# Weight parts in three steps, with the power of two moved into the casts, and shifted event times, in a fused gated-linear-attention and squared-ReLU kernel

## The chip, the cores and the metric

The kernel runs on one NeuronCore of a Trainium2 chip. The metric is device time in microseconds for one execution; a row of runs gives a median. The profile shown is of one execution of its own. TensorE does the matmuls, VectorE (DVE) and ScalarE (ACT) the elementwise work, SyncE (SP) issues all DMAs.

## The reference

Four batches of eight heads run a recurrence over 768 steps with a 48 x 48 state per head; the outputs of the eight heads side by side are the 384 columns of x (3072 tokens), which goes through a feed-forward layer with squared ReLU. q, k, v and alpha are float32; the two weight matrices come as 64-bit floats, which the kernel turns into float32 itself (L153 to L182, `first`, `middle`, `second`).

```python
state = alpha[:, :, t, :, None] * state + np.einsum('bhd,bhe->bhde', k[:, :, t], v[:, :, t])
y[:, :, t] = np.einsum('bhd,bhde->bhe', q[:, :, t], state)
...
x = np.ascontiguousarray(attn_out.transpose(0, 2, 1, 3)).reshape(B * S, H * D)
...
h = np.maximum(x @ w_in, 0.0)       # 384 -> 2048
return (h * h @ w_out)              # 2048 -> 384
```

## The kernel before

**Work.** The sequence is cut into chunks of 128 steps. A block is one chunk of one batch: 24 blocks. Four blocks (one chunk of all batches) make a group of 512 tokens: groups 0 to 5. Attention is done for two blocks at a time ("a pair"), in a chunked form: logs of alpha (`ln`), their split into two fp32r parts (`sp`), a cumulative sum by matmul (`cs`), exponentials (`eb`, `ei`), products with q and k (`mq`, `mk`), transposes on TensorE (`turn`), copies to SBUF (`qc`, `kc`), then `ga` and `gb`: scores, state sums, masks (`am`), new states (`us`, `st`, lines 406 to 421) and the outputs y of the pair before. `bl` writes the last row of the decay to DRAM and `br` reads it back turned, as `last`, which L421 needs.

**Feed-forward in three fp32r passes.** Group 0 uses plain float32 matmuls for its first layer and most of its second. From then on each operand is split in two parts, and three passes replace one float32 product. With E = 2^-12 and NEAR = 1 - 2^-13, a weight piece W (128 x 768 words, 8 pieces `i` of w_in, 8 pieces `o` of w_out) becomes b = fp32r(W NEAR) on ScalarE (`cast_w`, L551), l = W - b on VectorE (`rest_w`, through `combine`, L547), l / E on ScalarE (`scale_w`, L565), d = b - l/E on VectorE (`diff_w`, L547). b stays in SBUF; l and d go to DRAM (`keep`, L556) and are read back for each later group (`pump`, L589). Of the activations, x or the hidden values, a = fp32r(x NEAR) on ScalarE and l = x - a on VectorE (`split_to`, L596 and L547), d = l - E a on VectorE (`diff_to`, L600). A sum in PSUM takes b a and l l, is scaled by 1 + E (or E times it is added later), and then takes d d.

In the first layer (`layer_in`) 16 slices j give `in_x(j)` (six matmuls) and, two slices later, `in_y(j)` (three). A string of letters says by j mod 4 where the rest of a slice is done: D is one activation that scales by E, an add and a squared ReLU on VectorE; A is scaling, ReLU and square on ScalarE; M is A with the square on VectorE. The second layer (`layer_out`) is a row of `out_x(n)` (eight matmuls) and `out_y`; in groups 0 and 1 a part of it is done with plain float32 weights (`out_plain`).

**Order.** The first 36 us are a written-out list of steps. From there on `weave` takes a list of units of TensorE's work, each with a cost (1.05 for `in_x`, 0.53 for `in_y`, 1.08 for `out_x`, 1 for `out_plain`), and a list of events with times in the same units; an event is issued ahead of the first unit that begins at or after its time. The table `AT` (L19) holds these times: `g0`, `g1`, `g` when a pair's attention begins (in groups 0, 1, later), `sc0` how far group 0's events are stretched, `ga`, `gb` their place within a pair, `w_first`, `w_in_at`, `w_in_by`, `o0`, `o2` when weight pieces are split, `wstep` the distance of the steps of one split, `gx`, `g0x`, `g1x`, `xs` the split of the next x, `s0`, `h0`, `h1`, `h1by` where splits of hidden values stand, `str1` when the reads of d pieces begin, `tp`, `tp1` the letters. Each engine runs its instructions in the order of issue. PSUM is one pool of eight banks for everything; weight pieces share 26 buffers of SBUF.

`prepare` makes the events of one piece:

```python
def prepare(at, w, p):
    step = AT["wstep"]
    fs = (cast_w, rest_w, scale_w, diff_w)
    return [(at + i * step, f, (w, p)) for i, f in enumerate(fs)]
```

Of the kernel before, what the change touches and what calls it, by code (L numbers as in the profile page):

```python
# [9 lines left out]
FP32 = mybir.dt.float32  # L10
FP32R = mybir.dt.float32r
U32 = mybir.dt.uint32
AF = mybir.ActivationFunctionType
ALU = mybir.AluOpType
# [1 line left out]


GB = 4
AT = {'evs': 0.4, 'lead': 4, 'post': 3, 'w_first': (46.0, 49.5, 53.0), 'wstep': 1.6, 'w_in_at': 2, 'w_in_by': 3.4, 'room1': 22, 'room': 25, 's0': 4, 'ahead': 6, 'late': 2, 'xs': 0.2, 'g0': (-0.5, 19.5, 28.0), 'sc0': (2.35, 2.35, 2.35), 'g1': (2.5, 19.5, 35.0), 'g': (2.2, 15.0), 'g1x': 50, 'gx': 46, 'g0x': 55.5, 'k0': 2, 'h0': 18, 'k1': 4, 'h1': 4, 'h1by': 2, 'evs0': 0.8, 'tp': 'ADMD', 'tp1': 'ADAD', 'split': 8, 'o0': (40, 47), 'o1': (), 'o2': (23, 26, 29, 35, 42, 36), 'str1': 24, 'ga': 10, 'gb': 12.5}  # L19


RUN = {0: 128, 32: 32, 64: 64, 96: 32}
# [3 lines left out]
def kernel(  # L26
# [12 lines left out]
    nc = tc.nc  # L39
# [44 lines left out]
    def wt(name, dt=FP32, shape=(KM, DF // NW)):  # L84
        return wt_pool.tile([128, *shape], dt, tag="wt", name=name)
# [161 lines left out]

    SPLIT = AT["split"]

# [279 lines left out]
    E = 2.0**-12  # L529
    NEAR = 1.0 - 2.0**-13  # L530
# [3 lines left out]
    whole = {"i": w_in, "o": w_out}  # L534
# [5 lines left out]
    here, todo, room = {}, [], [22]  # L540
# [4 lines left out]
    def combine(steps):  # L545
        for o, x, op, z in steps:
            nc.vector.tensor_tensor(out=o, in0=x, in1=z, op=op)  # L547

    def cast_w(w, p):
        b = here["b", w, p] = wt("wb", FP32R, shapes[w])  # L550
        nc.scalar.activation(out=b, in_=whole[w][p], func=AF.Copy, scale=NEAR)  # L551

    made, stored, cut = {}, set(), set()

    def keep(x, w, p):
        nc.sync.dma_start(out=kept_parts[x, w, p], in_=words(made[x, w, p]))  # L556
        stored.add((x, w, p))

    def rest_w(w, p):
        l = made["l", w, p] = wt("wl", FP32R, shapes[w])  # L560
        combine(((l, whole[w][p], ALU.subtract, here["b", w, p].bitcast(FP32)),))

    def scale_w(w, p):
        l = made["l", w, p]
        nc.scalar.activation(out=l, in_=l.bitcast(FP32), func=AF.Copy, scale=1.0 / E)  # L565
        keep("l", w, p)

    def diff_w(w, p):
        b, l = here["b", w, p].bitcast(FP32), made["l", w, p].bitcast(FP32)
        d = made["d", w, p] = wt("wd", FP32R, shapes[w])  # L570
        cut.add((w, p))
        combine(((d, b, ALU.subtract, l),))
        keep("d", w, p)
        for x in "ld":
            t = made.pop((x, w, p))
            if w == "i" or p >= NW - AT["k0"] or (x == "l" and p >= NW - AT["k1"]):
                here[x, w, p] = t
        pump()

    def prepare(at, w, p):  # L580
        step = AT["wstep"]
        fs = (cast_w, rest_w, scale_w, diff_w)
        return [(at + i * step, f, (w, p)) for i, f in enumerate(fs)]

    def pump():
        while todo and todo[0] in stored and len(here) + len(made) + 2 * NW - len(cut) < room[0]:
            key = todo.pop(0)
            here[key] = wt("w" + key[0], FP32R, shapes[key[1]])
            nc.sync.dma_start(out=words(here[key]), in_=kept_parts[key])  # L589
# [3 lines left out]
        pump()  # L593

    def split_to(a, l, x):
        nc.scalar.activation(out=a, in_=x, func=AF.Copy, scale=NEAR)  # L596
        combine(((l, x, ALU.subtract, a.bitcast(FP32)),))

    def diff_to(d, a, l):
        nc.vector.scalar_tensor_tensor(  # L600
            out=d, in0=a.bitcast(FP32), scalar=-E, in1=l.bitcast(FP32), op0=ALU.mult, op1=ALU.add
        )

    def raw_r(name):
        return raw_pool.tile([128, KM, GB * C], FP32R, tag="raw", name=name)
# [3 lines left out]
    def split_x(g, kk):  # L609
        if kk == 0:  # L610
            x_parts["x"], x_parts["a"], x_parts["l"] = xT.pop(g), raw_r("xa"), raw_r("xl")
        split_to(x_parts["a"][:, kk], x_parts["l"][:, kk], x_parts["x"][kk])

    def diff_x(g, kk):
        if kk == 0:
            x_parts["d"] = raw_r("xd")
        diff_to(*(x_parts[k][:, kk] for k in "dal"))
# [44 lines left out]
    def splits_of_x(at, g):  # L662
        return [(at + i * AT["xs"], f, (g, i % KM)) for i, f in enumerate((split_x,) * KM + (diff_x,) * KM)]

    def layer_in(g):
        units = []
        for n in range(NJ + 2):
            if n < NJ:
                units.append((1.05, in_x, (n,)))
            if 0 <= n - 2 < NJ:  # L670
                units.append((0.53, in_y, (n - 2,)))
            if 0 <= n - AT["post"] < NJ:
                units.append((0, in_post, (n - AT["post"],)))
            if AT["lead"] <= n < AT["lead"] + AHEAD and (g > 1 or AT["k1"] == NW):
# [6 lines left out]
    def split_h(n, i):  # L681
        r = i % (AHEAD + MORE)
        if r < AHEAD:
            a, l = two_k("ha", FP32R), two_k("hl", FP32R)
        else:
            if i == AHEAD:
                extra[:] = [raw_r("hx") for _ in range(3)]
            x = 2 * (r - AHEAD)
            a, l = (extra[y // 3][:, y % 3] for y in (x, x + 1))
        split_to(a, l, hid.pop(n))  # L690
        h_parts[n] = a, l

    def diff_h(n):
        h_diff[n] = two_k("hd", FP32R)
        diff_to(h_diff[n], *h_parts[n])
# [250 lines left out]
    for p, at in enumerate(AT["w_first"]):  # L946
        events += prepare(at, "i", p)
# [6 lines left out]
    for p, at in enumerate(AT["o0"]):  # L954
        events += prepare(at, "o", order[p])
# [18 lines left out]
    for g in range(1, NG):  # L974
        events = []
        if g + 1 < NG:
            n = GB * (g + 1) + 2
            *ts, t0, t1 = AT["g1" if g == 1 else "g"]
            pairs = [(t, n - 2, False) for t in ts] + [(t0, n, True), (t1, n + 2, True)]
            events += attention(pairs, 1)  # L980
            events += splits_of_x(AT["g1x" if g == 1 else "gx"], g + 1)
        if g == 1:
            m = len(AT["w_first"])
            for p in range(m, NW):
                events += prepare(AT["w_in_at"] + AT["w_in_by"] * (p - m), "i", p)
            for i, at in enumerate(AT["o1"] + AT["o2"]):
                events += prepare(at, "o", order[len(AT["o0"]) + i])
            n = min(AT["k0"], AT["k1"])
            todo.extend(("l", "o", p) for p in range(NW - n, NW))
            events.append((AT["str1"], stream_out, (AT["k1"], "d")))  # L990
        kinds[0] = AT["tp1" if g == 1 else "tp"]
        room[0] = AT["room1" if g == 1 else "room"]
        events.append((26, stream, (g + 1,)))
        events.sort(key=lambda x: x[0])
        weave(layer_in(g) + layer_out(g), events)
        if g == 1:
            w_out.clear()
            hid.clear()
            acc.clear()
# [30 lines left out]
```

## Time and profile before

| | |
|---|---|
| median of 3 runs | 523.02 us (522.5 to 523.05) |
| span of the profiled execution | 520.6 us |
| granted TensorE clock | 1.000 |
| ScalarE scaling of `wl`, L565 | 16 x 847 ns, 13.5 us |
| ScalarE cast of weights, L551 | 16, 13.4 us |
| VectorE `wl` and `wd`, L547 | 32, 30.4 us |
| ScalarE `xa`, `ha`, `hx`, L596 | 91, 53.6 us |
| group 1, about 128 to 217 us | VectorE busy 14 to 18 of 20 us in its stages, ScalarE 8 to 18 |

The lines of the page give the busy time of an engine, the mean of one instruction, and the idle time ahead of it with what ended it. A line number can be that of a helper: L547 is `combine`, whoever calls it. "issue" is idle time for which the profile shows no cause.

### The profile page before, as it was taken

The numbers are of one execution on the slowest core, as the hardware profiler recorded it, in microseconds if no ns is written. First come the engines' busy times: TensorE is split into PE (matmuls) and PEld (weight loads), VectorE is DVE, ScalarE is ACT, GpSimd is POOL, SyncE is SP. The second block draws the span as 40 slices with busy tenths as digits, with TensorE's granted clock in tenths as the row PEclk, the third lists the DMA queues.
The fourth block names the chain that finished last, engine by engine and source line by source line (L and its number), as shares of the span: only waits on it lengthen the run. The fifth ranks groups of instructions, "written<-read, shape, count | busy, mean of one in ns | idle before, by whom it ended". The sixth has DMA issues, their size and how long they took to land.

```text
span 520.6 us, 12925 instructions
## 1 busy us (share of the span) xinstructions
PE 510.8 (98%) x5276; PEld 418.2 (80%) x5276; DVE 366.0 (70%) x631; ACT 313.0 (60%) x650; POOL 5.4 (1%) x29
## 2 busy tenths in 40 slices
PE   7989999999999999999999999999999999999997
PEld 4754455668887668988899988899988899988997
DVE  4798989979978787867597476587465476363861
ACT  4668785677888594575963275963275763164620
POOL 4000000000000000000000000000000000000000
PEclk9999999999999999999999999999999999999999
DMA  9999687244686787898884788964673534898201
GB/s 161 209 278 213 196 240 218 60 114 176 224 200 196 195 246 198 264 317 206 195 248 148 251 246 198 230 187 150 231 255 126 179 126 151 268 340 293 70 0 62
DMA packets 140995, 102.36 MB, mean 197 GB/s; under 512 B 111476, under 2 KB 114568, under 8 KB 140936
## 3 DMA queue, kind: packets, MB, share of 16 engines
q1 hardware_dynamic: 140936, 101.53, 68.3%
q8 instruction: 42, 0.69, 0.6%
q14 instruction: 17, 0.14, 0.1%
HBM read 84.18 MB, written 17.33 MB: 195 GB/s over the span
## 4 chain that ended last, share of the span: by engine, by line
PE 93%; DVE 2%; SPq 2%; DMA 1%; issue 1%; POOL 1%; ACT 0%; POOLq 0%; DVEq 0%
PE o L701 41%; PE h L622 32%; PE h L805 7%; PE y L352 4%; PE T L482 2%; PE sckv L372 2%; PE sckv L395 2%; PE cs L265 1%; DMA qk_lent<-in_q_dram 1%; SPq L303 1%; SPq L109 1%; PE cs L268 1%; PE cs L269 1%; DVE x L515 0%; DVE w_in L182 0%
## 5 line engine op out<-in xcount | busy, mean ns | idle before, releaser
L622 PE MATMUL h<-xa,wb 128*128 128x512 f32 x240 | 68.2, 392 | 0.0
L622 PE MATMUL h<-xl,wl 128*128 128x512 f32 x240 | 67.9, 391 | 0.0
L622 PE MATMUL h<-xd,wd 128*128 128x512 f32 x240 | 67.3, 396 | 0.0
L515 ACT COPY x<-y 32x256 f32<-32x256 f32 (+2 forms) x132 | 47.2, 366 | 25.4 <-PE y L352 20.1
L547 DVE TENSOR_TENSOR hid<-h,hid 128x512 f32<-128x512 f32 x40 | 27.6, 689 | 45.5 <-PE h L622 45.4
L701 PE MATMUL o<-wb,ha 128*128 128x384 f32 x160 | 54.6, 342 | 0.0
L701 PE MATMUL o<-w_out,hid 128*128 128x384 f32 x160 | 54.0, 491 | 0.0
L701 PE MATMUL o<-wd,hd 128*128 128x384 f32 x304 | 53.8, 334 | 0.0
L701 PE MATMUL o<-wl,hl 128*128 128x384 f32 x160 | 53.5, 335 | 0.0
L639 ACT ACTIVATE h<-h 128x512 f32<-128x512 f32 x40 | 23.3, 582 | 49.7 <-PE h L622 49.7
L622 PEld LDWEIGHTS h<-xl,wl 128*128 128x128 f32 x240 | 45.1, 188 | 10.0 <-DVE xl L547 0.4
L701 PEld LDWEIGHTS o<-wd,hd 128*128 128x128 f32 x304 | 52.7, 188 | 0.3 <-DVE osb L737 0.3
L622 PEld LDWEIGHTS h<-xa,wb 128*128 128x128 f32 x240 | 44.6, 188 | 9.3 <-ACT xa L596 0.2
L622 PEld LDWEIGHTS h<-xd,wd 128*128 128x128 f32 x240 | 44.2, 188 | 9.2
L701 PE MATMUL o<-wb,hx 128*128 128x384 f32 x144 | 48.7, 338 | 0.0
L701 PE MATMUL o<-wl,hx 128*128 128x384 f32 x144 | 48.1, 334 | 0.0
L701 PEld LDWEIGHTS o<-w_out,hid 128*128 128x128 f32 x160 | 29.8, 190 | 19.3
L637 ACT ACTIVATE hid<-h 128x512 f32<-128x512 f32 x40 | 24.0, 600 | 34.6 <-PE h L622 34.5
L805 PE MATMUL h<-x,w_in 128*128 128x512 f32 (+1 forms) x108 | 43.6, 552 | 1.2 <-ACT x L515 1.2
L596 ACT ACTIVATE ha<-hid 128x512 fp32r<-128x512 f32 x40 | 25.6, 639 | 25.5 <-DVE hx L547 16.1
L805 PEld LDWEIGHTS h<-x,w_in 128*128 128x128 f32 x108 | 19.9, 190 | 21.1 <-issue 17.2
L547 DVE TENSOR_TENSOR hl<-hid,ha 128x512 fp32r<-128x512 f32 x40 | 27.5, 688 | 10.1 <-ACT ha L596 10.1
(114 smaller groups left out, 879.7 us busy)
## 6 DMA issues: line engine op xcount, KB each, us to landing
wd<-do SPq DMA_DIRECT2D x36, 384.0 KB, 3.7
wl<-lo SPq DMA_DIRECT2D x34, 384.0 KB, 4.0
wl<-li SPq DMA_DIRECT2D x32, 384.0 KB, 3.5
wd<-di SPq DMA_DIRECT2D x32, 384.0 KB, 3.9
raw<-in_moe_w_in_dram SPq DMA_DIRECT2D x8, 768.0 KB, 5.6
raw<-in_moe_w_out_dram SPq DMA_DIRECT2D x8, 768.0 KB, 5.6
v_in<-in_v_dram SPq DMA_DIRECT2D x24, 192.0 KB, 4.7
out_dram<-osb SPq DMA_DIRECT2D x24, 192.0 KB, 1.9
```

The costliest lines, as they stand in the source:

```text
L352: ins = nc.tensor.matmul(out=ys[e][64 * half : 64 * half + D + G * e, m % 2, p // 2, t], lhsT=lhsT, rhs=rhs, start=(half, e) not in seen, ...
L372: nc.tensor.matmul(out=ps[e][HALF[h], 0, p, :], lhsT=ks[rows, p, HALF[h]], rhs=qs[rows, p, HALF[h]], start=True, stop=True, skip_group_che ...
L395: nc.tensor.matmul(out=ps[h][64 * e : 64 * (e + 1), 1, p, G:64], lhsT=tile_of("k", n)[HALF[h], 2 * p + e, :], rhs=tiles["v"][n % NV][HALF[ ...
L482: nc.tensor.transpose(out=ps[h][:, i, p, :], in_=rows[HALF[h], 128 * p : 128 * (p + 1)], identity=ident[HALF[h], HALF[h]],)
L515: copy(out=x[kk][to : to + m, t : t + 2], in_=blk[n]["y"][e][r : r + m, :, p // 2],)
L547: nc.vector.tensor_tensor(out=o, in0=x, in1=z, op=op)
L596: nc.scalar.activation(out=a, in_=x, func=AF.Copy, scale=NEAR)
L622: nc.tensor.matmul(out=acc["h", j], lhsT=here[w, "i", p][:, kk, jj * 128 : (jj + 1) * 128], rhs=x_parts[x][:, kk], start=start and kk == 0 ...
L637: nc.scalar.activation(out=hid[j], in_=x, func=AF.Copy, scale=E)
L639: nc.scalar.activation(out=x, in_=x, func=AF.Copy, scale=1.0 + E)
L701: nc.tensor.matmul(out=acc[t][:, 0:DM], lhsT=lhs[:, t * C : (t + 1) * C], rhs=rhs, start=start, stop=stop, skip_group_check=True,)
L805: nc.tensor.matmul(out=ps, lhsT=w[:, kk, c0 : c0 + 128], rhs=xT[g][kk][:, cols], start=(kk == 0), stop=(kk == KM - 1),)
```

## The change

The factor 1/E moves into the casts, so that no scaling is left on ScalarE: b is cast from W NEAR / E, l = W / E - b and d = l - E b are each one SCALAR_TENSOR_TENSOR on VectorE. To fit, the activations' a is cast from x NEAR E, l = x - a / E becomes a SCALAR_TENSOR_TENSOR, and d = a - l a TENSOR_TENSOR. A weight piece is split in three events, 1.35 units apart, not four 1.6 apart. Nearly all times in `AT` change, among them the order in which pieces 0 and 1 of w_in are split; group 1's letters go from ADAD to ADMD, those of later groups from ADMD to DMAD.

```diff
--- before.py
+++ after.py
@@ -16,7 +16,7 @@
 
 
 GB = 4
-AT = {'evs': 0.4, 'lead': 4, 'post': 3, 'w_first': (46.0, 49.5, 53.0), 'wstep': 1.6, 'w_in_at': 2, 'w_in_by': 3.4, 'room1': 22, 'room': 25, 's0': 4, 'ahead': 6, 'late': 2, 'xs': 0.2, 'g0': (-0.5, 19.5, 28.0), 'sc0': (2.35, 2.35, 2.35), 'g1': (2.5, 19.5, 35.0), 'g': (2.2, 15.0), 'g1x': 50, 'gx': 46, 'g0x': 55.5, 'k0': 2, 'h0': 18, 'k1': 4, 'h1': 4, 'h1by': 2, 'evs0': 0.8, 'tp': 'ADMD', 'tp1': 'ADAD', 'split': 8, 'o0': (40, 47), 'o1': (), 'o2': (23, 26, 29, 35, 42, 36), 'str1': 24, 'ga': 10, 'gb': 12.5}
+AT = {'evs': 0.4, 'lead': 4, 'post': 3, 'w_first': (43.69, 37.36, 56.81), 'wstep': 1.35, 'w_in_at': 2.4, 'w_in_by': 3.87, 'room1': 22, 'room': 25, 's0': 3, 'ahead': 6, 'late': 2, 'xs': 0.26, 'g0': (-0.55, 19.56, 28.31), 'sc0': (2.35, 2.26, 2.35), 'g1': (2.9, 15.48, 34.89), 'g': (1.95, 18.67), 'g1x': 50.57, 'gx': 43.81, 'g0x': 55.38, 'k0': 2, 'h0': 15, 'k1': 4, 'h1': 3, 'h1by': 5, 'evs0': 0.51, 'tp': 'DMAD', 'tp1': 'ADMD', 'split': 8, 'o0': (44.47, 50.43), 'o1': (), 'o2': (28.87, 27.52, 29.94, 28.82, 42.72, 38.72), 'str1': 19.38, 'ga': 9.32, 'gb': 12.53}
 
 
 RUN = {0: 128, 32: 32, 64: 64, 96: 32}
@@ -548,7 +548,7 @@
 
     def cast_w(w, p):
         b = here["b", w, p] = wt("wb", FP32R, shapes[w])
-        nc.scalar.activation(out=b, in_=whole[w][p], func=AF.Copy, scale=NEAR)
+        nc.scalar.activation(out=b, in_=whole[w][p], func=AF.Copy, scale=NEAR / E)
 
     made, stored, cut = {}, set(), set()
 
@@ -558,18 +558,19 @@
 
     def rest_w(w, p):
         l = made["l", w, p] = wt("wl", FP32R, shapes[w])
-        combine(((l, whole[w][p], ALU.subtract, here["b", w, p].bitcast(FP32)),))
-
-    def scale_w(w, p):
-        l = made["l", w, p]
-        nc.scalar.activation(out=l, in_=l.bitcast(FP32), func=AF.Copy, scale=1.0 / E)
+        nc.vector.scalar_tensor_tensor(
+            out=l, in0=whole[w][p], scalar=1.0 / E, in1=here["b", w, p].bitcast(FP32),
+            op0=ALU.mult, op1=ALU.subtract,
+        )
         keep("l", w, p)
 
     def diff_w(w, p):
         b, l = here["b", w, p].bitcast(FP32), made["l", w, p].bitcast(FP32)
         d = made["d", w, p] = wt("wd", FP32R, shapes[w])
         cut.add((w, p))
-        combine(((d, b, ALU.subtract, l),))
+        nc.vector.scalar_tensor_tensor(
+            out=d, in0=b, scalar=-E, in1=l, op0=ALU.mult, op1=ALU.add
+        )
         keep("d", w, p)
         for x in "ld":
             t = made.pop((x, w, p))
@@ -579,7 +580,7 @@
 
     def prepare(at, w, p):
         step = AT["wstep"]
-        fs = (cast_w, rest_w, scale_w, diff_w)
+        fs = (cast_w, rest_w, diff_w)
         return [(at + i * step, f, (w, p)) for i, f in enumerate(fs)]
 
     def pump():
@@ -593,13 +594,13 @@
         pump()
 
     def split_to(a, l, x):
-        nc.scalar.activation(out=a, in_=x, func=AF.Copy, scale=NEAR)
-        combine(((l, x, ALU.subtract, a.bitcast(FP32)),))
+        nc.scalar.activation(out=a, in_=x, func=AF.Copy, scale=NEAR * E)
+        nc.vector.scalar_tensor_tensor(
+            out=l, in0=a.bitcast(FP32), scalar=-1.0 / E, in1=x, op0=ALU.mult, op1=ALU.add
+        )
 
     def diff_to(d, a, l):
-        nc.vector.scalar_tensor_tensor(
-            out=d, in0=a.bitcast(FP32), scalar=-E, in1=l.bitcast(FP32), op0=ALU.mult, op1=ALU.add
-        )
+        combine(((d, a.bitcast(FP32), ALU.subtract, l.bitcast(FP32)),))
 
     def raw_r(name):
         return raw_pool.tile([128, KM, GB * C], FP32R, tag="raw", name=name)
```

## The prediction

> **What bounds the kernel now.** I read the page first: busy times, clock, the chain that ended last.
>
> ```profile
> PE 510.8 (98%) x5276; PEld 418.2 (80%) x5276; DVE 366.0 (70%) x631; ACT 313.0 (60%) x650; POOL 5.4 (1%) x29
> ...
> PEclk9999999999999999999999999999999999999999
> ...
> PE 93%; DVE 2%; SPq 2%; DMA 1%; issue 1%; POOL 1%; ACT 0%; POOLq 0%; DVEq 0%
> ```
>
> TensorE is busy for 98% of the span at full clock, and 93% of the chain is its matmuls. The change removes no matmul: the instruction order of both kernels holds the same matmuls, in another order. So what can be won is TensorE's idle time and its hidden slow starts. The waits of TensorE come next.
>
> ```profile
> PE h L805 <- ACT x L515: 1.2, 3, 0.7
> PE warm L221 <- POOL s L67: 1.1, 1, 1.1
> PE y L352 <- issue: 1.0, 1, 1.0
> PE sckv L395 <- DMA v_in<-in_v_dram: 0.8, 2, 0.4
> PE kT L309 <- DVE k_in L284: 0.7, 1, 0.7
> ```
>
> Columns: total us, times, longest. In the table of stages TensorE idles 3.34 us in 0:20, 1.94 in 20:40, 0.96 in 200:220, 3.5 at the end, and nothing to speak of between. The first 36 us and the last 3 come from the written-out start list and from the output's way home; in both kernels the orders of all engines there are the same. What is left is the row "issue", 1.0 us. The timeline around it:
>
> ```profile
> 202.45 0.64 PE L352 MATMUL y<-am,v_in 64*48 64x64 f32 x27
> ...
> 204.05 0.33 PE L352 MATMUL y<-am,v_in 64*48 64x64 f32 x3 [0.96 <-issue]
> ```
>
> TensorE stops inside the third `ga` of group 1 and waits for nothing that the profile names. Beyond that, a pitch longer than its neighbours shows hidden waits: two `h<-xl,wl` starts near 128.6 come 0.1 us late each (xl, behind ScalarE), and one T start at 141.75 comes 0.23 late (the last `q_in` product on VectorE ends at 141.96).
>
> **Part by part.**
>
> *The arithmetic.* Sixteen `wl` activations on ScalarE (L565, 847 ns, 13.5 us) go. The twelve ops that follow keep their engine and length: TENSOR_TENSOR `wl` 951 ns and SCALAR_TENSOR_TENSOR of the same 128x768 956 ns; for 128x512 688 against 692. So rest and difference swap forms at no cost, bounded by the 4 ns of these rows, and only ScalarE is relieved. ScalarE is 60% busy and 0% of the chain: worth 0 on the path, except at the split of x. There `xa` stands behind four output copies and one of the removed activations (127.86); without it the two late `xl` starts go: **-0.2**, bounds -0.2 and 0.
>
> *Kinds of squares.* ADAD to ADMD in group 1 moves four squares from ScalarE (632 ns) to VectorE (682): +2.7 us of VectorE in group 1. ADMD to DMAD only rotates the same kinds. No cost by itself; it fills VectorE's queue, below.
>
> *Order of TensorE.* Counting runs of matmuls in both orders: group 1's second score run (`ga`) moves from between `o<-w_out` matmuls to the seam of the two layers, so one change between attention and fp32r matmuls is saved. A change is worth what the timeline shows at 308.93 to 311.67: three `xl` take 0.77 up to the T start for 3 x 0.227, three `xd` behind it 0.81 for 0.68, so 0.22, and some 0.03 in T's own end: **-0.25**, bounds -0.3 and 0. Elsewhere the number of changes is equal.
>
> *The stop at 203.* The page has 42 packets of 0.69 MB on the instruction queue, 16.4 KB each; TensorE's 10,552 records over 42 are 251 a packet. I read the stop as a block of code that landed late: within that `ga` 32 records with their 32 loads start in 0.46 us, so 256 take 1.9. It needs one block to begin and end within the burst of some 320 records. By the order, 8 pairs of `o` matmuls (32 records with their loads) fewer stand between the turn and this `ga`, and other `ga` move by 12 to 48 records. Of eight such bursts one stopped, so each has a chance near 0.1. I take the stop as gone, **-1.0**, bounds -1.2 (its whole pitch) and +1.2 (two bursts stop).
> The Trainium skill (Runtime: NRT & Kernel Launch, Instruction fetch mechanics) has blocks of 256 instructions, which the packet size agrees with, but says that crossing one is mostly hidden, as dispatch is slower than the fill; by that the stop is something else and may well stay, which makes the sum 1.0 longer (the second rival).
>
> *VectorE's queue in group 1's first layer.* This is the price of the change. The second pair's attention starts at unit 15.48, not 19.5 (a unit is 1.36/1.05 = 1.3 us there), so its logs' parts, its `k` and `q` products and its turn fall into the stretch in which five weight parts are still made. Starts that follow each other in the timeline give the lengths:
>
> ```profile
> 135.02 0.95 DVE L547 TENSOR_TENSOR wl<-w_in,wb 128x768 fp32r<-128x768 f32 x1
> 135.89 0.68 DVE L547 TENSOR_TENSOR hid<-h,hid 128x512 f32<-128x512 f32 x1
> 136.49 0.55 DVE L284 TENSOR_TENSOR k_in<-k_in,inv 128x384 f32<-128x384 f32 x1
> 136.96 0.95 DVE L547 TENSOR_TENSOR wd<-wb,wl 128x768 fp32r<-128x768 f32 x1
> ...
> 148.98 0.36 DVE L420 TENSOR_TENSOR s<-sckv,us 128x192 f32<-128x192 f32 x1
> 150.46 0.36 DVE L421 TENSOR_TENSOR s<-s,last 128x192 f32<-128x192 f32 x1 [1.12 <-DMA last<-row]
> 150.73 0.68 DVE L651 SCALAR_TENSOR_TENSOR hid<-hid 128x512 f32<-128x512 f32 x1
> ```
>
> 768 wide 0.87, 512 wide 0.60, 384 wide 0.47. From the end of the first score products (147.70) to 150.73 a mask and state run takes 3.03 with its wait for `last`; the next, without a wait, 1.72 (153.67 to 155.39). In the changed order VectorE has from there to the last `q` product ahead of the second turn: 3.03 + 1.72, four of 768 (3.48), six of 512 (3.62), two log splits (0.87 each), four of 384 (1.96 to the last one's end): 15.55 us. TensorE has 54 `h` matmuls x 0.227, 1.0 of scores, 0.7 of `cs`, 0.9 of T and some 0.5 of changes: 15.35. In the kernel before 72 `h` and two `o` stand there, 5 us more. So the turn is late by 0.2 and its semaphore, and the `cs` ahead of it by about as much: I take **+0.4**. The first turn loses too: `cs` moves behind one `in_x` (1.36 us) while T stays, and VectorE, whose queue from the last `osb` on now also holds the early weight part, ends the last `q` product about 142.45 against a T that wants it at 141.75: 0.7 where 0.23 stood, **+0.4**. Each is bounded by 0 (VectorE need not be full) and by the longest wait for `last` in the trace, 2.0, in the place of the 1.1 counted.
>
> *Later groups.* First `ga` at 9.32 instead of 10 comes one `in_x` (1.36) earlier after the turn. Its `qs` copies ended 2.4 us ahead of it (312.77, 315.20), so 1.0 stays. `last` now comes later against it: in group 2 VectorE waited 2.04 until 240.64, and the `hid` add behind it freed a bank at 242.23 for a matmul at 242.91. One more square stands ahead of that add now (0.60): 0.1 is left. **0**, bounds 0 and 0.3 in each of three groups. The second pair comes 3.67 units later, the split of x 2.2 units earlier (46 to 43.81); the last copies of `y` are at 32.4, so there are 11 units between.
>
> *SyncE.* The stores of `wl` are now issued from `rest_w`, without ScalarE between; the loads of `last` keep their place behind the loads of `q`, which wait for the turn; in group 1's third pair a `do` store that waits for VectorE stands between them. No TensorE wait on a weight load is near: the streams run ten and more us ahead in both orders. Cost 0; without that lead a 384 KB load costs its 3.5 to 4 us.
>
> Sum on the profiled span: 520.6 - 1.0 - 0.25 - 0.2 + 0.4 + 0.4 = 519.95. The median of the runs, 523.02, is 2.4 above this span; I add 2.4: **522.4**.
>
> **Rivals.** (1) VectorE keeps up in group 1 (ScalarE's 13.5 us feed it earlier): the two +0.4 go and the 0.23 at 141.75 too: 521.3. For it: VectorE idles 1.76 ahead of the mask at 147.92; against it: the sum above has no idle time left. (2) A code stop stays or comes elsewhere: 523.4. For it: the stop is one sample, its cause is not named by the profile; against it: seven like bursts ran through. (3) Slower: `last` becomes the bound in group 1. Its four loads are issued behind the `q` loads and landed 8.2 us after the turn (142.25 to 150.46); the second pair's `ga` now comes one `h` run after the turn, 4.1 us instead of 5.5. VectorE would wait 2 to 2.5 there and at the first pair, and with no slack in the queue (15.55 to 15.35) the wait passes to TensorE as soon as it exceeds the 1.1 counted: +1.3 at each of two turns, 525.0. Against it: in the second pair before there was no wait for `last`. (4) That the scaling isn't gone: excluded, the order has no such activation.
>
> **Chances.** Forecast 0.42, first rival 0.30, code stop 0.12, `last` 0.16. Within 0.2% (1.05 us, about what a measurement here can tell from no change) lie the code stop and most of the forecast; some of the forecast's low side falls under 521.97. Faster 0.38, same 0.41, slower 0.21. The range reaches from just below the first rival, 521.0, to 524.6, which leaves out the worse half of the third and little else.
>
> **What would show it.** Right: no L565 row, ScalarE near 297 us busy, no "issue" wait in a `y` run, late T starts of 0.3 to 0.8 in group 1 only, groups 2 to 5 unchanged in length (79.2 us from one group to the next). Wrong: a TensorE wait on DVE `q_in`, `hi` or `lo` of over 1 us in 130 to 200; a wait for `last` of over 2 us on DVE; a new "issue" stop; any wait of TensorE on weight loads.

## The result, and the profile after

The changed kernel takes 521.18 us (median of 8 runs, 520.68 to 522.40) against 523.03 (8 runs, 522.50 to 524.56): ratio 0.9966, 95% interval 0.9954 to 0.9977. The profiled execution has a span of 518.9 us where the kernel before had 520.6, the granted TensorE clock is 1.000 in both. It lies inside the forecast's range, and nearer to the first rival (521.3) than to the forecast itself (522.4).

The busy times and the chain that ended last, from the page after:

```profile
PE 509.3 (98%) x5276; PEld 417.9 (81%) x5276; DVE 368.7 (71%) x635; ACT 299.6 (58%) x630; POOL 5.3 (1%) x29
...
PE 93%; DMA 4%; DVE 1%; SPq 1%; ACT 1%; issue 0%; DVEq 0%
```

TensorE's waits after (total us, times, longest):

```profile
PE kT L309 <- DVE k_in L284: 1.3, 1, 1.3
PE h L806 <- ACT x L515: 1.2, 3, 0.7
PE warm L221 <- POOL s L67: 1.1, 1, 1.1
PE sckv L395 <- DMA v_in<-in_v_dram: 1.0, 2, 0.8
```

ScalarE is 13.4 us less busy, TensorE 1.5; "issue" is gone from TensorE's waits, and those that are left lie in the first 36 us. Where the time went is read from the same TensorE instruction in both timelines:

| instruction | before | after | gained so far |
|---|---|---|---|
| first o of three passes, end of group 0 | 120.28 | 120.28 | 0 |
| first xd behind group 1's first turn | 142.40 | 141.62 | 0.78 |
| first xd behind group 1's second scores | 153.20 | 152.41 | 0.79 |
| first o behind group 1's third turn | 196.12 | 195.72 | 0.40 |
| first o behind the third `ga` (after: 201.22, and 1.38 for the eight o matmuls that now follow it) | 204.31 | 202.60 | 1.71 |
| end of the last matmul | 517.08 | 515.34 | 1.74 |

So there are three places: 0.78 won by the end of the first turn, 0.39 lost between 153 and 196, 1.31 won at the stop; from then on nothing.

**The first place.** ScalarE's timeline ahead of the split of x (start, length, line, operation), before:

```profile
121.46 0.84 ACT L565 ACTIVATE wl<-wl 128x768 fp32r<-128x768 f32 x1
122.21 0.83 ACT L551 ACTIVATE wb<-w_in 128x768 fp32r<-128x768 f32 x1
122.94 3.32 ACT L515 COPY x<-y 64x256 f32<-64x256 f32 x9
126.28 1.68 ACT L596 ACTIVATE xa<-x 128x512 fp32r<-128x512 f32 x3
127.86 0.83 ACT L565 ACTIVATE wl<-wl 128x768 fp32r<-128x768 f32 x1
```

and after:

```profile
120.41 4.37 ACT L515 COPY x<-y 32x256 f32<-32x256 f32 x12 [0.51 <-PE y L352]
124.81 1.67 ACT L597 ACTIVATE xa<-x 128x512 fp32r<-128x512 f32 x3
126.39 0.83 ACT L551 ACTIVATE wb<-w_in 128x768 fp32r<-128x768 f32 x1
```

A scaling and a cast stood among the copies of x; without them `xa` starts 1.47 earlier, and VectorE's queue behind it too. The late `xl` starts go: 0.26 of the 0.78. As much again is won on either side of the split: ahead of it by the same scaling's absence, behind it by that of another. From the timelines before, of VectorE, TensorE's weight loads, ScalarE and VectorE:

```profile
122.34 0.96 DVE L547 TENSOR_TENSOR wd<-wb,wl 128x768 fp32r<-128x768 f32 x1 [0.29 <-ACT wl L565]
124.69 2.75 PEld L701 LDWEIGHTS o<-wd,hd 128*128 128x128 f32 x16 [0.28 <-DVE osb L737]
136.02 0.85 ACT L565 ACTIVATE wl<-wl 128x768 fp32r<-128x768 f32 x1
139.55 0.48 ACT L280 ACTIVATE inv<-cs 128x384 f32<-128x384 f32 x1
140.06 0.56 DVE L284 TENSOR_TENSOR k_in<-k_in,inv 128x384 f32<-128x384 f32 x1 [1.08 <-ACT inv L280]
```

VectorE's `wd` waited for the scaling at 121.46, and the `osb` operations behind it freed the banks for `o<-wd,hd`, the last matmuls of group 0, late. The first `h` of group 1 starts at 127.60, and at 127.33 after, 0.27 earlier. At the turn the scaling at 136.02 stood in ScalarE's queue ahead of the second `inv`, for which VectorE idled 1.08 us; after, it doesn't idle there, and the last `q_in` product ends at 141.17 for a T start at 141.27, where before it came 0.23 late. That is the last 0.25.

**The second place.** The same 454 matmuls stand between 153 and 196 in both. `cs` takes 0.19 and T 0.18 more; `h` takes 0.32 more and `o<-w_out` 0.29 less. The second turn stood inside `o<-w_out` and now stands inside `h`, and the scores run stands at the end of `h`; each edge between attention and one of the two costs 0.09 to 0.11 in either stream. VectorE's timeline and TensorE's, after:

```profile
161.13 0.55 DVE L284 TENSOR_TENSOR q_in<-q_in,b 128x384 f32<-128x384 f32 x1
161.59 0.55 DVE L284 TENSOR_TENSOR k_in<-k_in,inv 128x384 f32<-128x384 f32 x1
162.06 0.55 DVE L284 TENSOR_TENSOR q_in<-q_in,b 128x384 f32<-128x384 f32 x1
```

```profile
162.28 0.42 PE L482 MATMUL T<-ident,k_in 64*128 64x64 f32 x8
162.67 0.46 PE L482 MATMUL T<-ident,q_in 64*128 64x64 f32 x8
```

Groups of eight T follow each other at 0.25 to 0.30; this one came 0.39 behind, and its `q_in` ended at 162.61.

**The third place.** TensorE's timeline in the third `ga`, after: 31 y matmul records without a break where 27 stood before the stop.

```profile
200.60 0.69 PE L352 MATMUL y<-am,v_in 64*48 64x64 f32 x31
201.22 0.44 PE L702 MATMUL o<-wb,hx 128*128 128x384 f32 x1
```

### The profile page after: what moved, and what is told of

Read it like the earlier page. It is cut to its first block, busy times and chain, and to the rows that moved or that the text cites. A ratio compares the mean times of both kernels' runs of the same rounds, so it can differ in the third digit from the quotient of the medians.

```text
span 518.9 us, 12889 instructions
## 1 busy us (share of the span) xinstructions
PE 509.3 (98%) x5276; PEld 417.9 (81%) x5276; DVE 368.7 (71%) x635; ACT 299.6 (58%) x630; POOL 5.3 (1%) x29
## 4 chain that ended last, share of the span: by engine, by line
PE 93%; DMA 4%; DVE 1%; SPq 1%; ACT 1%; issue 0%; DVEq 0%
PE o L702 41%; PE h L623 32%; PE h L806 7%; PE y L352 4%; PE T L482 2%; PE sckv L372 2%; PE sckv L395 2%; DMA a_in<-in_alpha_dram 1%; DMA a_lent<-in_alpha_dram 1%; DMA k_in<-in_k_dram 1%; PE cs L265 1%; DMA row<-b 1%; PE cs L269 1%; DVE x L515 1%; PE cs L268 1%; SPq L109 0%
## 5 line engine op out<-in xcount | busy, mean ns | idle before, releaser
L597 ACT ACTIVATE ha<-hid 128x512 fp32r<-128x512 f32 x40 | 25.2, 638 | 17.2 <-DVE hl L598 10.8
L547 DVE TENSOR_TENSOR osb<-o,osb 128x384 f32<-128x384 f32 x24 | 12.9, 553 | 25.8 <-PE o L702 24.6
```

What stands on the lines that cost most here:

```text
L597: nc.scalar.activation(out=a, in_=x, func=AF.Copy, scale=NEAR * E)
```

## The experiments

Ratios are to the kernel before, run alongside. The first stretch of 36 us varies by up to 1 us from one execution to the next in kernels that are alike there; where traces are compared, positions are taken from the start of the first long attention run (99.16 before, 99.15 after).

**1 and 2. Each half alone.** `e1_arith` is the new arithmetic with all of the old table; `e2_at9` the old arithmetic with the new table (and `'wstep': 0.9`, so that the last of four steps stands where the last of three did). TensorE's instruction order is exactly that of before and of after.

> New arithmetic alone: three steps for each weight part, the factors in the casts, and every time and letter of the kernel before. TensorE's instruction order is exactly that of the kernel before. My theory: the stop of TensorE at 203 us depends only on where the long attention run stands in TensorE's instruction stream, so it stays (pitch about 1.2 us there, shown as an issue wait of 1.0); what ScalarE gives back is the split of x in front of group 1 and the late T start behind it, 0.5 + 0.2, nothing after: 522.3 us, ratio 0.9985. Rival A (the stop came from a queue that the scaling activations had filled): the stop goes too, 521.3, ratio 0.9967. Rival B (ScalarE's relief is worth nothing on the path, the split of x is set by the orders): 523.0, ratio 1.000.

> New times and letters alone, with the old arithmetic (four steps, the scaling on ScalarE; steps 0.9 units apart, so that the last step of a part stands where the changed kernel has its last of three). TensorE's instruction order is exactly that of the changed kernel. My theory: no stop at 203 (-1.0), the saved change of forms at group 1's seam (-0.25), but sixteen activations of 0.85 us are back on ScalarE, one of them close to the split of x: 0.5 to 0.8 of the changed kernel's gain goes, 521.9 us, ratio 0.998. Rival A (stop tied to ScalarE): a stop of about 1 us somewhere in group 1, 522.9. Rival B (the scaling is needed to make room for the second pair at 15.48): T and cs starts of group 1's second turn late by 1 us or more, 523 or above.

| | old table | new table |
|---|---|---|
| old arithmetic | 1 | 1.0047 (1.0035 to 1.0060), 525.08 us |
| new arithmetic | 0.9987 (0.9979 to 0.9996), 522.05 us | 0.9966 (0.9954 to 0.9977), 521.18 us |

The first came as expected: its execution begins 0.93 later, and its first `xd` behind the turn at 142.56 less 0.93 is 141.63, the whole 0.78 without the table; the stop at 203 stays (1.07), and one of 0.41 comes at 176.5. The second did not: the new table alone makes the kernel slower. By parts that add up, the two would give 1.0034; together they give 0.9966, 0.68% or 3.6 us better. Rival B was the nearer one, but the place was the first turn, not the second. There TensorE stops 1.6 us for a scaled bank, and 1.5 us more are lost among the T of the turn. ScalarE's timeline and VectorE's in `e2_at9`:

```profile
126.86 0.83 ACT L551 ACTIVATE wb<-w_in 128x768 fp32r<-128x768 f32 x1
131.94 0.84 ACT L565 ACTIVATE wl<-wl 128x768 fp32r<-128x768 f32 x1 [4.25 <-DVE wl L547]
132.81 0.58 ACT L639 ACTIVATE h<-h 128x512 f32<-128x512 f32 x1
```

```profile
130.96 0.95 DVE L547 TENSOR_TENSOR wl<-w_in,wb 128x768 fp32r<-128x768 f32 x1
```

ScalarE had nothing to do for 4.25 us: the scaling at the head of its queue waits for a rest that VectorE reaches at 130.96, and the first `h` activation, which the changed kernel does at 128.92, stands behind it.

**3 and 4. The place in the instruction stream.** Six fp32 matmuls of 16 columns (n = 6 once, 24 records) behind the first warm-up matmul, in the kernel before and in the changed one.

```diff
+        for _ in range(n):
+            nc.tensor.matmul(out=ps[:, 0, 0:16], lhsT=lhsT, rhs=s_t[0][:, 0, 0:16], start=True, stop=True)
```

> Kernel before, with six more fp32 matmuls of 16 columns behind the first warm-up matmul, where TensorE waits for the first loads: 24 more records ahead of everything else, no other change. My theory (a block of instructions that arrives late, so that the place of the long run in the stream decides): the run at 200.5 starts at record 157 instead of 133 of a block of 256 and has no stop; 522.0 us, ratio 0.998; the other seven runs move to 26, 180, 3, 225, 74, 40 and 82 and have none either. Rival (the stop has another cause, data or VectorE in group 1): stop of 1.0 stays at 203, 523.0, ratio 1.000.

> Changed kernel with the same six small matmuls at the start. My theory: the long runs at 167.4 and 198.7 us start at records 112 and 111 of a block of 256 in the changed kernel and move to 136 and 135, next to the 133 at which the kernel before stopped: an issue wait of about 1.0 us in each, 523.2 us against 521.2 of the changed kernel, ratio 1.000 to the kernel before (one stop: 522.2). Rival (the stop has another cause): no issue wait, 521.2, ratio 0.9966.

Measured: 1.0005 (0.9996 to 1.0015) and 1.0062 (1.0049 to 1.0076). The matmuls were not free: TensorE is 2.1 us later at the first long run in both, which the expectations had left out. Apart from that, in the traces, the kernel before gained 1.1 (of the stop at 203, a gap of 1.17, one of 0.19 is left) and the changed kernel lost 3.3. The changed kernel's waits and its timeline:

```profile
PE y L353 <- issue: 2.6, 3, 1.5
```

```profile
171.25 0.69 PE L353 MATMUL y<-am,v_in 64*48 64x64 f32 x27
173.41 0.33 PE L353 MATMUL y<-am,v_in 64*48 64x64 f32 x4 [1.47 <-issue]
...
204.39 0.66 PE L353 MATMUL y<-am,v_in 64*48 64x64 f32 x27
205.91 0.33 PE L353 MATMUL y<-am,v_in 64*48 64x64 f32 x4 [0.87 <-issue]
```

Both stops that were forecast are there, and a third of 0.44 in group 2 that wasn't. The rival falls: nothing else was changed.

**5 and 6. The same without its cost.** Nine fillers of 256 columns in the start become eighteen of 128 (w is NP // 2; 36 records more), in the kernel before (`before_halves`) and with the new arithmetic (`e1_halves`).

```diff
-                rhs=s_t[3], start=True, stop=True,
+                rhs=s_t[3][:, 0:w], start=True, stop=True,
```

> Kernel before, with nine start-up filler matmuls of 256 columns made into eighteen of 128 columns: the same columns, 36 records more ahead of all that follows, TensorE busy there anyway. My theory: the stop always falls at the record that is 192 in a block of 256, when the long run begins some 290 to 320 records ahead of it; the run at 200.5 now begins at 169, the others at 38, 192, 15, 237, 86, 52 and 94, and none stops (237 is the doubtful one: 239 lost 0.44 once). The start costs nothing: 521.8 us, ratio 0.9976, no issue wait. Rival (the stop is only moved, the instruction stream is as late somewhere else): 523.0, ratio 1.000.

> New arithmetic with every time and letter of the kernel before, and the same eighteen half-wide fillers. My theory: the arithmetic's 0.8 stays, the stops of 1.07 at 203 and 0.41 at 176 go (runs begin at 190 and 166), and the late starts of 0.37 that the changed kernel has at the second turn of group 1 aren't there: 520.6 us, ratio 0.9953, a little faster than the changed kernel (0.9966). Rival (the moved times are worth something by themselves beyond the stop): not faster than the changed kernel, 521.2 or above.

The first: 0.9976 (0.9966 to 0.9986), 521.64 us, no "issue". This is the stop by itself, 1.26 us. The second: 0.9967 (0.9955 to 0.9979), as fast as the changed kernel and not faster, so the expectation fails. With the stops gone and the old table, the new arithmetic gives all that the changed kernel gives: beyond the stop, no gain of the moved times can be measured. The stops of 1.07 and 0.41 are gone, but 0.46 is lost in group 2, on VectorE and then on TensorE:

```profile
239.84 0.36 DVE L422 TENSOR_TENSOR s<-s,last 128x192 f32<-128x192 f32 x1 [3.12 <-DMA last<-row]
```

```profile
241.46 0.98 PE L624 MATMUL h<-xa,wb 128*128 128x512 f32 x3 [0.36 <-DVE hid L548]
```

TensorE is 1.9 us further by then than in the kernel before, the last row only 0.9, and the add that frees a bank stands behind it.

**7. VectorE's squares.** The changed kernel with `'tp1': 'ADAD'`.

> Changed kernel with the letters ADAD in group 1 as before: four squares of 0.68 us go from VectorE to ScalarE, TensorE's order unchanged. My theory: the late starts of cs and T at 157 and 162 (0.37 us in all) come from VectorE's full queue, so they go: 520.8 us, ratio 0.9959. Rival (ScalarE, with 0.6 us more for each of these squares, becomes the one that is late): the late starts stay or grow to 1 us, 521.2 to 522, and named by ACT.

Measured: 0.9967 (0.9954 to 0.9979), which tells nothing apart. The trace does: all `cs` and T of group 1's second pair are on time, and the stretch from the second scores to the third turn takes 42.97 instead of 43.31 us. But two things are gone from VectorE's queue there: one square (0.60) between the scores and the turn, and the wait for the last row, 1.31 in the changed kernel and none here. The letters have a part in the second too: ahead of the first turn, one square less stands before a `wd` whose store SyncE issues ahead of the rows' loads, and these go out 0.57 earlier. So 0.34 is the price of both together; the run doesn't separate them.

**8. The blocked scaling, earlier.** `e2_at9` with `w_first` (43.69, 37.36, 53.0).

> The new times with the old arithmetic again, but the third early weight part at 53.0 units, as before, in place of 56.81; TensorE's order is unchanged. My theory: in the run with 56.81 the scaling activation stood in ScalarE's queue behind a rest that VectorE made 4.25 us later, and held back the first h activation, for which TensorE stopped 1.77 us at 131.5; with the part earlier the stop goes, the lateness of T at 143 (1.5 us) only in part: 523.3 us, ratio 1.0005. Rival (sheer load of ScalarE, wherever the activation stands): 524.5 to 525, ratio 1.004.

Measured: 1.0038 (1.0026 to 1.0051), 525.19 us: the expectation fails. ScalarE no longer waits there, but cast and scaling now stand ahead of `xa`, 1.5 us, and `wd` ahead of the third `xl`; TensorE loses 1.6 us there instead. Moving the step moved the loss.

**9 and 10. Waiting and load apart.** The changed kernel with a fourth step again (0.9 apart): `after_hop` copies one column of l on ScalarE and stores l only behind that, `after_load` copies all of wb into the tile of d.

```diff
+        nc.scalar.activation(out=flat(l)[:, 0:1], in_=words(l)[:, 0:1], func=AF.Copy, scale=1.0)
```

```diff
+        nc.scalar.activation(out=d, in_=here["b", w, p].bitcast(FP32), func=AF.Copy, scale=1.0)
```

> Changed kernel with a fourth step again between rest and difference, 0.9 units apart as in the run that had the new times with the old arithmetic, but this step copies one column of the rest onto itself on ScalarE: ScalarE waits for VectorE's rest and VectorE's difference waits for ScalarE as in the old arithmetic, at next to no load. TensorE's order is that of the changed kernel. The new times with the old arithmetic lost 3.9 us to the changed kernel. My theory: more than half of it is the wait, since ScalarE takes its instructions in order and the first h activation stood 3 us behind a rest that wasn't made: 523.4 us, ratio 1.0007. Rival (load alone, sixteen times 0.85 us): under 0.5 lost, 521.5, ratio 0.997.

> Changed kernel with a fourth step in the same place that copies the whole wb (128x768) on ScalarE into the tile that the difference is then written to: the load of the old scaling, but ScalarE waits for no VectorE rest (the difference still waits for the copy). TensorE's order is that of the changed kernel. My theory: less than half of the 3.9 us, 522.6 us, ratio 0.999. Rival (load alone): all of it, 525, ratio 1.004.

Measured: 1.0006 (0.9998 to 1.0015), 523.23 us, and 0.9986 (0.9977 to 0.9995), 522.19 us: close to the theory, and "load alone" falls. ScalarE's timeline in the two:

```profile
126.52 0.83 ACT L551 ACTIVATE wb<-w_in 128x768 fp32r<-128x768 f32 x1
131.70 0.20 ACT L568 ACTIVATE wl<-wl 128x1 fp32r<-128x1 f32 x1 [4.35 <-DVE wl L561]
131.92 0.58 ACT L646 ACTIVATE h<-h 128x512 f32<-128x512 f32 x1
```

```profile
127.02 0.83 ACT L551 ACTIVATE wb<-w_in 128x768 fp32r<-128x768 f32 x1
127.88 0.85 ACT L569 ACTIVATE wd<-wb 128x768 fp32r<-128x768 f32 x1
129.31 0.58 ACT L644 ACTIVATE h<-h 128x512 f32<-128x512 f32 x1 [0.58 <-PE h L627]
```

Sixteen instructions of 0.20 us cost 2.1 us of the kernel ((1.0006 - 0.9966) x 523), sixteen of 0.85 that wait for no rest 1.0. The traces show that the two figures don't add up to the 4.2 by which the old arithmetic is slower under this table, since they share a part. Up to the first `xd` of group 1 (131.45 in the changed kernel), where one of the short ones had held ScalarE for 4.35, `after_hop` loses 0.98 and `after_load` 0.03. From there to the end of the turn both lose, 1.01 and 0.76: in both, VectorE has a `wl`, for whose cast it waits 0.34, ahead of two more products of q and k than in the changed kernel, which the shorter step of 0.9 brings. So the wait at the head of the queue is what costs at the first place. How much of the second is the step and how much ScalarE's fourth instruction isn't shown; a run of three steps 0.9 apart, which would tell, was not made.

**11 and 12. The rows' loads ahead of the loads of q**, in `e1_halves` and in `after_adad`.

```diff
-        (6.5, "turn br1"),
-        (7.0, "kc0 qc0 kc1 qc1 br0"),
+        (6.5, "br1 br0 turn"),
+        (7.0, "kc0 qc0 kc1 qc1"),
```

> New arithmetic, all times of the kernel before, half-wide fillers, and the loads of the last rows issued ahead of the turn's loads of q instead of behind them; TensorE's order unchanged. Without this move VectorE waited 3.1 us for the last row in group 2 and TensorE 0.4 us for the bank that the add behind it frees (0.46 in all). My theory: the rows land 1 us earlier, VectorE's wait is near 2.0, TensorE's is gone: 520.7 us, ratio 0.9957. Rival (the rows' loads are slow from the traffic of the weight streams, not from their place in the queue): wait stays at 3, 521.1, ratio 0.9967.

> Changed kernel with ADAD in group 1 and the loads of the last rows ahead of the loads of q. In the changed kernel VectorE's wait for the last row (2.5 us at most) reaches no TensorE instruction. My theory: nothing gained over ADAD alone by the trace, 520.9 us, ratio 0.996; both together the fastest version so far or equal to it. Rival (the loads of q, now behind the rows, come late for group 2's products): 521.5 or above, with a wait named q_in DMA.

Measured: 0.9968 (0.9957 to 0.9980) and 0.9964 (0.9952 to 0.9977). In the first VectorE's waits for the last rows fall from 10.8 us in all to 1.1, and TensorE's wait in group 2 is gone, so the place in the queue it was. The time doesn't show it (0.9957 was expected, the very edge of the interval): a stop of 0.16 stands at 240.88, and the profiled execution began 0.8 later. The second is within the intervals of the changed kernel. No version was found that is measurably faster than the changed kernel.

## Why the prediction was right and wrong, step by step

- **The stop, -1.0: right, and shown.** Measured 1.31 in the trace and 1.26 by `before_halves`. Its cause is the place. Counted in the traces, TensorE's matmuls, weight loads and semaphore instructions in the order of their starts, every stop of over 0.1 us in a dense run behind the first 36 us lies at a record that is 192 in a block of 256 (4544 before; 3776 and 4544 in `e1_arith`; 4544 in `before_shift6`; 3776, 4544 and 5312 in `after_shift6`; one of 0.13 and one of 0.16 in the two `e1_halves` runs).
- **How the stop comes about, as far as the traces show.** Some 2.3 to 2.6 us before TensorE goes on behind the longer ones, a packet begins on the instruction queue; in slow stretches such packets begin about record 157 at the earliest, some 290 records ahead of the place. Attention starts 320 records in 2.37 us, so 290 take 2.1: 0.2 to 0.5 too little. That happens when a run still lasts at the place, 256 + 192 = 448 records behind the block's start, and begins ahead of the packet: between 128 (448 - 320) and about 157. The five that began at 130 to 154 all stopped, the one at 156 didn't, the one at 157 lost 0.19, and those at 111 to 113 and from 166 to 237 didn't stop. Two things stay open: in the four stops of over 1 us the packet itself began 0.9 to 1.3 us after TensorE had passed record 157, and the 0.44 at a run that began at 239 is outside the rule. That the changed kernel escapes was a matter of chances in the prediction and not worked out: its two runs in group 1 begin at 112 and 111, some 16 records short of a stop. The second rival, a stop that stays or comes elsewhere, falls: the changed kernel has none. The Trainium skill (Runtime: NRT & Kernel Launch, Instruction fetch mechanics) calls a crossing mostly hidden: it is at most of the some forty in each kernel, but not here, where one cost 1.26 us.
- **The arithmetic, 0 on the path but -0.2: the step that failed.** "ScalarE is 60% busy and 0% of the chain: worth 0 on the path" took the removed step for 13.5 us of load beside the path. What counts is what stands behind a scaling in the queues of ScalarE and of VectorE. It is worth 0.78 by the first turn with the old table (`e1_arith`), 0.26 at each of three places: the banks of `o<-wd,hd` in group 0, the split of x, and the turn. Only the split was in the sum, and at about its size. The activation named for it, at 127.86, stands behind `xa`, though; the one ahead is at 121.46.
- **VectorE's first turn, +0.4: wrong in sign**, -0.25 came. I had placed VectorE's queue at the times it had before, among them its 1.08 of waiting for the `inv` behind a scaling; in `e1_arith`, in the old order, 0.54 of that wait is left, and in the changed kernel nothing. With it the first rival's "ScalarE feeds it earlier" was right.
- **VectorE's second turn, +0.4: right.** 0.37 measured (0.19 `cs`, 0.18 T), 0.34 of it gone with ADAD, which also took out VectorE's wait of 1.31 for the last row.
- **The seam, -0.25: wrong, 0.** The turn and the scores run have their edges in both kernels, 0.32 more in `h` against 0.29 less in `o<-w_out`. The change that is saved is the direct one from `h` to `o<-w_out`, and it cost nothing: the starts around it in the trace before (166.34) follow at 0.23 and 0.32 like their neighbours.
- **Later groups and SyncE, 0: right** (0.03). VectorE's waits for the last row grew from 4.6 to 6.2 us, longest 2.5, and reached no TensorE instruction. The prediction had named a wait of over 2 us there as a sign of being wrong, though the kernel before has one of 2.04 already. The third rival's wait cost 0.46 in `e1_halves`, in the old order with TensorE 1.9 us further.
- **What the working left out**: that the new table rests on the new arithmetic. I costed both as independent edits; the table alone is 0.47% slower, the pair 0.34% faster.

Terms against measured: -1.0, -0.25, -0.2, +0.4, +0.4 make -0.65; -1.31, 0, -0.53 (0.27 of it in `o<-wd,hd`), -0.25, +0.37 make -1.72, and 1.74 is the difference. That the time came out by the first rival, whose terms make -1.68, is in part luck: it holds the seam's -0.25, which did not come, and leaves out the second turn's 0.37, which did.

## What to carry to other kernels

An engine that is 60% busy and off the chain can still set the time at a seam: look at what stands in its queue ahead of the seam, and whether that waits for another engine. A step on ScalarE that waits for VectorE can cost by the wait at the head of the queue and not by its length (at the same place 0.98 us with the wait and 0.03 without). When a step is taken out, move all queues that follow it before pricing the next edit. And when a dense run of small matmuls stops without a cause, count instructions to it: a few more ahead of it, where they cost nothing, can be worth most of the edit (here 1.26 of 1.78 us).

## What the runs showed of the hardware that was not expected

- A stop of TensorE of 0.13 to 1.69 us in a run of records some 7 ns apart can be put in or taken out by 24 to 36 records hundreds of microseconds earlier.
- Matmuls of 16 columns weren't small at the start: twelve passes took 2.4 us, 200 ns each, with weights of 128 x 128 loaded for each. Eighteen fillers of 128 columns took about as long as nine of 256 (4.18 us in `before_halves` against 4.05).
- Two activations on ScalarE, at 121.46 and 136.02, made TensorE 0.78 us late by 142.40, and TensorE's waits name neither: they show only as starts less than 0.3 late. The chain of waits, which is read back from the end, shows 0% for ScalarE before and 1% after.
